# Another order of the heads in the first attention, and another quarter of V kept in SBUF

## The chip, the cores and the metric

The kernel runs on one core of a Trainium2 chip. The metric is the time of one execution on the device, in microseconds (us).

## The reference

Four tokens (B = 4, one position each, D = 512) go through two layers, each an attention with a cached K and V and a gated feed-forward block. Both layers use the same weights and the same cache:

```python
x = x + A(layernorm(x)); x = x + B(layernorm(x))     # first layer
x = x + A(layernorm(x)); x = x + B(layernorm(x))     # second layer

def A(x):      # 32 query heads in groups of 4 on 8 KV heads, Dh = 128, the last W = 2048 positions
    q = x @ wq
    o = softmax(q k^T * Dh ** -0.5) @ v
    return o @ wo
def B(x):      # F = 1792
    return (sigmoid(x @ w_gate) * (x @ w_up)) @ w_down
```

K of one KV head, for all four batches, is 2 MB in bf16, and so is V. wq and wo are 4 MB each, the three weights of B 1.75 MB each.

## The kernel before, in words

The program is written as a plan (`_Plan`): each operation names its engine, an estimated length, and what it reads and writes. `_schedule` then puts the operations of each engine in a fixed order by running the plan with these estimates: at each step it takes, among the operations that could start within 60 ns of the earliest one, the one that stands first in the program. The issues of DMAs (all on SP, line 461) keep the order of the program. `_assign_sync` turns the dependencies into semaphore waits. On the chip each engine runs its list in order, and so an instruction that waits holds up all that stand behind it on its engine.

SBUF is filled by hand. A place is written as (buffer, first unit, units); a unit is 256 bf16 values in each of 128 partitions, 64 KB. The buffers are:

- `kt`: K of all eight heads, 32 units each (256 units). It is read from memory once, transposed in place by TensorE and copied back (lines 736 and 746), and used by both layers.
- `ws` (`wo_sb`): wo, 8 units per head, kept for both layers.
- `ar` (`arena`, 75 units) and `sx` (`side`, 31 units): everything that streams, V, wq and the weights of B, and parts of these that stay.

`WHERE` says which places each load takes; names are `V0_h` for V of head h in the first attention, `V2_h` in the second, `g`, `u` and `d` for the gate, up and down weights, `q01` for the half of wq that is read twice.

**First attention** (layer 0). The loop goes over `HEADS1`. For each head it transposes K of the next one, makes the scores (`scores`, line 759), softmax (maximum line 768, exponential line 781, transpose of the result lines 787 and 792), the product with V (`pv_wo`) and the product with wo (line 947). V of head h lies in the arena in one of two slots of 32 units, units 42 to 73 and units 0 to 31, in turns. In the last place of the order, V comes in three pieces.

**Feed-forward block** (`glu`). Its gate weights and the second reading of wq need room in `ws`, where wo lies. So `stash` copies 16 units of wo into four PSUM banks (VectorE, line 994), and copies them back (ScalarE, line 990) before the second attention uses them.

**Second attention** (layer 2). K is in `kt` already. V is read again, except for pieces that are still where the first attention left them: `VKEEP` names, for a head, the unit of its V at which such a piece starts, and `load_v` leaves out its DMA and puts it first in the list of pieces of the product. Before: for head 6 its last quarter (8 units, in arena units 66 to 73), and for head 7 its last 6 units (arena units 30 to 35). V of heads 0 and 1 goes to free parts of the arena and `side`. V of heads 2 to 7 overwrites K in `kt`, from the bottom up: the load of V of head 2 waits for the scores of head 0, and so on, two heads behind. The loop `for n, h in enumerate(HEADS2)` makes the scores of head n, issues the load of V of head n + 1, does the product with V and wo of head n - 2 (`v2_head`), and spreads the softmax weights of head n.

The product with V has two forms. In `WIDE` places (heads 2 to 5 in the second attention) it is one group of 32 matmuls of 256 columns (line 852), copied out by ScalarE (line 860) and summed by TensorE (line 867); it needs the whole of V. In the others (heads 0, 1, 6 and 7) it is 64 matmuls of 32 columns (line 895), one group for each piece of V, so that a piece can be used as soon as it is there.

After the second attention comes the last `glu`, whose down weights lie in the arena (`d0_3`), in `kt` behind V of head 7 (`d4_3`, `d8_3`) and in `side` (`d12_3`), and the output.

Of the kernel before, what the change touches and what calls it, by code (L numbers as in the profile page):

```python
# [268 lines left out]
def build(nc, A_x, A_k, A_v, A_wq, A_wo, B_wg, B_wu, B_wd, out):  # L269
# [4 lines left out]
    _, HKV, SK, DH = A_k.shape  # L274
# [23 lines left out]
    UHEAD = NB * UBLK  # L298
    KEEPG = 4
    GU = F // UNIT  # L300
# [4 lines left out]
    AHEAD = 2  # L305
    NWR = 7
    WIDE = {0: {0: 4, 1: 4, 2: 4, 3: 4, 4: 4, 5: 4, 6: 2}, 2: {2: 2, 3: 2, 4: 2, 5: 2}}
    VKEEP = {6: 24, 7: 26}
    HEADS1 = list(range(HKV))
    HEADS2 = list(range(HKV))  # L310

    SCRATCH = 256
# [10 lines left out]
    NS = (low - SIDE) // (2 * UNIT)  # L323
# [15 lines left out]
    with es:  # L339
        def sb(name, shape, dt):  # L340
            return es.enter_context(nc.sbuf_tensor(name, shape, dt))

        kt = sb("kt", [128, HKV * NB * BLK], BF16)
# [12 lines left out]
        pb = sb("pb", [128, 4 * UNIT], BF16)  # L356
# [48 lines left out]
        def blk_ap(s):  # L405
            return {"kt": kt, "ws": wo_sb, "ar": arena, "pt": pt, "pb": pb, "sx": side}[s[0]][:, s[1] * UNIT:(s[1] + s[2]) * UNIT]

        def blk_tok(s):
            return tuple((s[0], u) for u in range(s[1], s[1] + s[2]))

        def kblk(h, b):
            return ("kt", (h * NB + b) * UBLK, UBLK)
# [6 lines left out]
        MAIN = WKEEP[2][0][1]  # L419
        G0 = MAIN - KEEPG * GU  # L420

        def ar(u, n):
            return ("ar", u, n)

        def sx(u, n):
            return ("sx", u, n)

        WHERE = {}
        for h in range(HKV - 1):
            WHERE["V0_%d" % h] = [ar(MAIN - UHEAD if h % 2 == 0 else 0, UHEAD)]  # L430
        WHERE["V0_%d" % (HKV - 1)] = [ar(0, 16), ar(16, 10), ar(30, 6)]
        WHERE["u01"], WHERE["g01"] = ar(52, 2 * GU), ar(38, 2 * GU)
        PT3 = ("kt", 187, 4)
        WHERE.update({
            "g23_1": ("ws", 0, 2 * GU), "u23_1": ar(0, 2 * GU),
            "d0_1": ar(14, 8), "d4_1": ar(22, 8), "d8_1": ar(36, 2), "d9_1": ("ws", 14, 2), "d10_1": ("pb", 0, 4),
            "d12_1": ("pt", 4, 4),
            "q01": [("ws", 0, 8), ar(0, 14), ar(14, 4), ("ws", 8, 6)],
            "V2_0": [ar(18, 12), ar(36, 2), sx(0, 16), sx(16, 2)],
            "V2_1": [sx(18, NS - 18), ar(0, 18), ar(74, 1)],  # L440
            "g23_3": ar(0, 2 * GU), "u23_3": sx(0, 2 * GU),
            "d0_3": ar(14, 8), "d4_3": ("kt", 179, 8), "d8_3": ("kt", 192, 8), "d12_3": sx(14, 4),
        })
        WHERE["V2_6"] = [("kt", 128, 24), ar(66, 8)]
        WHERE["V2_7"] = [("kt", 152, 16), ("kt", 168, 10), ar(30, 6)]
        for h in range(2, HKV - 2):
            WHERE["V2_%d" % h] = [("kt", (h - 2) * UHEAD, UHEAD)]

        def bankb(b):
            return ps[:, b, :].bitcast(BF16)  # L450
# [7 lines left out]
        def dma(name, dst, src, w, r=(), rate="bw_4k", nbytes=None, sem=None):  # L458
            if nbytes is None:
                nbytes = dst.partition_size() * dst.free_nbytes()  # L460
            o = P.op("sync", name, 0.0, lambda e, dst=dst, src=src: e.dma_start(dst, src),
                     r=r, w=w, dma_bytes=nbytes, dma_rate=tm[rate])
            if sem is not None:
                o.sem = sem
                o.inc = 16
            return o

        def load_v(L, h):
# [3 lines left out]
            for s in WHERE["V%d_%d" % (L, h)]:  # L472
                n = s[2]
                if L == 2 and VKEEP.get(h) == u0:
                    got.insert(0, (s, u0 * UNIT // 128))
# [247 lines left out]
        def k_head(h, banks):  # L723


            base = h * NB * BLK
            for t in range(UBLK):
                bank, ev = banks[tcount[0] % len(banks)]
                tcount[0] += 1

                def e_tr(pe, t=t, bank=bank):
                    last = None
                    for v in range(2):
                        for q in range(NB):
                            c0 = base + (q * NJ + 2 * t + v) * 128
                            last = pe.transpose(bankb(bank)[:, (v * NB + q) * 128:(v * NB + q + 1) * 128],  # L736
                                                kt[:, c0:c0 + 128], ident_b[:, :])
                    return last
                tok = [("kt", (h * NB + b) * UBLK + t) for b in range(NB)]
                P.op("tensor", "T%d_%d" % (h, t), 8 * tm["pe_tr"], e_tr,  # L740
                     r=tok + [("ident_b",)], w=[("pst", bank)], banks=(bank,))

                def e_ev(e, ev=ev, t=t, bank=bank):
                    to = kt[:, base:base + NB * BLK].rearrange("p (b y) -> p b y", b=NB)[:, :, t * UNIT:(t + 1) * UNIT]
                    fr = bankb(bank)[:, 0:NB * UNIT].rearrange("p (y b) -> p b y", b=NB)
                    return (e.tensor_copy if ev == "vector" else e.copy)(to, fr)  # L746
                P.op(ev, "evT%d_%d" % (h, t), 1300.0 if ev == "vector" else 1100.0, e_ev,
                     r=[("pst", bank)], w=tok, banks=(bank,))
# [231 lines left out]
                 r=[("pswt",), ("xT",)], w=[("xT",)], banks=(MB,))  # L980

        GB, UB, YB = 0, 1, 2
        STASH = ((0, 3), (4, 0), (8, 1), (12, 2))

        def stash(back):
            for u, b in STASH if back else STASH[1:] + STASH[:1]:
                at = blk_ap(("ws", u, 4))
                r, w = [("wo", u * UNIT // WOH)], [("st", b)]
                if back:
                    P.op("scalar", "back%d" % u, 1010.0, lambda a, b=b, at=at: a.copy(at, bankb(b)), r=w,  # L990
                         w=r + list(blk_tok(("ws", u, 4))), banks=(b,))
                else:
                    P.op("vector", "stash%d" % u, 620.0,
                         lambda v, b=b, at=at: v.tensor_scalar(ps[:, b, :].bitcast(I32), at.bitcast(I32), 0, None, ALU.bitwise_or),
                         r=r, w=w + [("pst", b), ("pss", b)] + list(blk_tok(("ws", u, 4))), banks=(b,))
# [142 lines left out]
        TBK = [(i % 3, "vector" if i % 8 in (1, 4, 7) else "scalar") for i in range(24)]  # L1138
# [19 lines left out]
        def load_k(h):  # L1158
            dma("K_%d" % h, kt[:, h * NB * BLK:(h + 1) * NB * BLK], k_d[h],
                w=[t for b in range(NB) for t in blk_tok(kblk(h, b))], rate="bw_16k", nbytes=NB * W * DH * 2)  # L1160
# [7 lines left out]
                dma("wo_%d" % h, to, A_wo[h * REP * 128:(h + 1) * REP * 128, :].rearrange("(p j) n -> p (j n)", j=4),  # L1168
                    w=[("wo", h)])

        load_k(0)
        k_head(0, TBK)
        pieces = []
        for ktc in range(2):
            s = ("kt", HKV * UHEAD - (2 - ktc) * 2 * UBLK, 2 * UBLK)
# [11 lines left out]
        for n in range(1, KLEAD):  # L1187
            load_k(HEADS1[n])
        for n, h in enumerate(HEADS1):
            if n + 1 < HKV:  # L1190
                k_head(HEADS1[n + 1], TBK)
            scores(0, n, h, 3, MB)
# [3 lines left out]
            if n + KLEAD < HKV:  # L1196
                load_k(HEADS1[n + KLEAD])
            if n == HKV - 1:
# [76 lines left out]
def bass_interleave_layers__sliding_block_cached__glu_gated_glu__decode_kernel(  # L1275
    nc, A_x, A_k_cache, A_v_cache, A_wq, A_wo, B_x, B_w_gate, B_w_up, B_w_down, out,
):
    build(nc, A_x, A_k_cache, A_v_cache, A_wq, A_wo, B_w_gate, B_w_up, B_w_down, out)
# [28 lines left out]
```

## Time and profile before

| what | us |
|---|---|
| median of 3 runs | 176.73 (176.54 to 176.75) |
| the profiled execution's own time | 177.9 |
| its span in the profile | 176.1 |
| TensorE (PE) busy | 136.4 |
| VectorE (DVE) busy | 99.7 |
| ScalarE (ACT) busy | 75.6 |
| first instruction of the second attention's scores (L759) | starts at 124.0 |
| output DMA issued | 173.9 |

Times in the views run from the start of the span. In rows of the timeline the columns are start, length (both us), engine, line of the kernel, operation, what it writes and reads, shapes, and how many instructions are merged; in brackets stands how long the engine was idle before, and what ended that. SPq stands for a DMA issue on SP. A row of the DMA issues gives the size and the median time from issue to landing. PEclk is the clock that was granted to TensorE, 1 being full.

### The profile page before, as it was taken

The numbers are of one execution on the slowest core, as the hardware profiler recorded it, in microseconds if no ns is written. First come the engines' busy times: TensorE is split into PE (matmuls) and PEld (weight loads), VectorE is DVE, ScalarE is ACT, GpSimd is POOL, SyncE is SP. The second block draws the span as 40 slices with busy tenths as digits, with TensorE's granted clock in tenths as the row PEclk, the third lists the DMA queues.
The fourth block names the chain that finished last, engine by engine and source line by source line (L and its number), as shares of the span: only waits on it lengthen the run. The fifth ranks groups of instructions, "written<-read, shape, count | busy, mean of one in ns | idle before, by whom it ended". The sixth has DMA issues, their size and how long they took to land.

```text
span 176.1 us, 4872 instructions
## 1 busy us (share of the span) xinstructions
PE 136.4 (77%) x2175; PEld 99.8 (57%) x2175; DVE 99.7 (57%) x246; ACT 75.6 (43%) x129; POOL 6.8 (4%) x17
## 2 busy tenths in 40 slices
PE   0394699898897878978977967459849796897794
PEld 0382398566385664665654657448227553675693
DVE  7453016969658576894797532104499888521440
ACT  2073227947287647292663040304455644430300
POOL 5200000000000000000000002002000000000020
PEclk9999557999999999999999555555599999655555
DMA  5999999999999999999999999999899999999930
GB/s 187 417 436 437 422 421 421 443 424 422 421 421 432 414 431 424 411 432 422 434 424 381 408 422 412 396 407 399 305 411 430 435 435 417 421 411 419 401 153 5
DMA packets 9504, 69.39 MB, mean 394 GB/s; under 512 B 1032, under 2 KB 2316, under 8 KB 6156
## 3 DMA queue, kind: packets, MB, share of 16 engines
q1 hardware_dynamic: 9476, 69.08, 94.8%
q8 instruction: 17, 0.28, 0.6%
q14 instruction: 3, 0.02, 0.0%
q10 hardware_dynamic: 8, 0.00, 0.0%
HBM read 69.08 MB, written 0.00 MB: 392 GB/s over the span
## 4 chain that ended last, share of the span: by engine, by line
DMA 62%; PE 29%; DVE 3%; ACT 3%; issue 1%; SPq 1%; DVEq 0%
DMA arena<-in_A_v_cache_dram 31%; DMA kt<-in_A_v_cache_dram 11%; DMA side<-in_A_wq_dram 9%; PE ps L852 6%; DMA wo_sb<-in_B_w_gate_dram 5%; DMA wo_sb<-in_A_wq_dram 5%; PE ps L759 4%; PE ps L736 4%; PE ps L1050 3%; PE ps L668 2%; PE ps L867 2%; PE ps L895 2%; PE ps L947 1%; ACT wo_sb L990 1%; PE ps L699 1%
## 5 line engine op out<-in xcount | busy, mean ns | idle before, releaser
L746 ACT COPY kt<-ps 128x1024 bf16<-128x1024 bf16 x40 | 39.1, 1018 | 25.7 <-PE ps L736 25.6
L736 PE MATMUL ps<-ident_r,kt 128*128 128x128 bf16 x512 | 38.5, 231 | 4.8 <-DMA kt<-in_A_k_cache_dram 2.6
L736 PEld LDWEIGHTS ps<-ident_r,kt 128*128 128x128 bf16 x512 | 32.7, 105 | 11.7 <-issue 4.4
L746 DVE COPY kt<-ps 128x1024 bf16<-128x1024 bf16 x24 | 29.2, 1215 | 12.5 <-PE ps L736 12.3
L759 PE MATMUL ps<-kt,qs 128*32 128x512 bf16 x256 | 18.0, 405 | 2.0 <-ACT pb L781 1.3
L817 DVE TENSOR_TENSOR pt<-ps,ofbr 128x1024 bf16<-128x1024 f32 (+1 forms) x15 | 15.5, 1031 | 2.9 <-PE ps L792 2.8
L852 PE MATMUL ps<-arena,pt 128*64 128x512 bf16 (+1 forms) x128 | 13.4, 391 | 4.3 <-DMA arena<-in_A_v_cache_dram 4.2
L768 DVE TENSOR_REDUCE nmz<-ps 128x1 f32<-128x512 f32 x16 | 11.0, 687 | 6.1 <-PE ps L759 5.9
L781 ACT ACTIVATE pb<-ps,nmz 128x512 bf16<-128x512 f32 x16 | 11.1, 693 | 7.2 <-DVE nmz L778 3.7
L787 DVE STREAM_TRANSPOSE pb<-pb 128x512 bf16<-128x512 bf16 x16 | 11.3, 704 | 4.4 <-ACT pb L781 4.2
L852 PEld LDWEIGHTS ps<-arena,pt 128*64 128x64 bf16 (+1 forms) x128 | 6.0, 117 | 9.7 <-DMA arena<-in_A_v_cache_dram 5.7
L759 PEld LDWEIGHTS ps<-kt,qs 128*32 128x32 bf16 x256 | 5.6, 100 | 7.7 <-ACT pb L781 1.9
L860 ACT COPY arena<-ps 128x512 f32<-128x512 f32 (+1 forms) x7 | 3.9, 556 | 13.8 <-PE ps L852 13.8
L824 ACT ACTIVATE pt<-ps,ofbr 128x96 bf16<-128x96 f32 x28 | 7.2, 342 | 5.4 <-PE ps L792 5.3
L630 POOL TENSOR_TENSOR rs<-pt,rs 128x4 f32<-128x4 f32 x4 | 4.1, 1014 | 119.9 <-DVE pt L626 119.9
L832 PE MATMUL ps<-rowf,nmz 128*128 128x16 f32 x32 | 6.8, 290 | 2.1 <-DVE pt L817 1.9
L947 PE MATMUL ps<-wo_sb,onr 128*16 128x512 bf16 x56 | 6.5, 457 | 2.0 <-DVE onr L939 2.0
L867 PEld LDWEIGHTS ps<-arena 128*128 128x128 f32 x52 | 6.7, 201 | 2.1 <-ACT arena L860 1.6
L867 PE MATMUL ps<-arena 128*128 128x16 f32 x52 | 7.4, 273 | 0.7 <-ACT arena L860 0.2
L1050 PE MATMUL ps<-xn,arena 128*128 128x5 bf16 (+1 forms) x168 | 6.3, 172 | 2.0 <-DMA arena<-in_B_w_up_dram 1.1
L832 PEld LDWEIGHTS ps<-rowf,nmz 128*128 128x128 f32 x32 | 5.4, 212 | 4.1 <-DVE pt L817 2.8
L990 ACT COPY wo_sb<-ps 128x1024 bf16<-128x1024 bf16 x4 | 4.0, 1012 | 8.3 <-DMA wo_sb<-in_A_wq_dram 8.3
(143 smaller groups left out, 161.1 us busy)
## 6 DMA issues: line engine op xcount, KB each, us to landing
kt<-in_A_k_cache_dram SPq DMA_DIRECT2D x8, 2048.0 KB, 24.5
arena<-in_A_v_cache_dram SPq DMA_DIRECT2D x7, 2048.0 KB, 20.2
kt<-in_A_v_cache_dram SPq DMA_DIRECT2D x4, 2048.0 KB, 18.3
wo_sb<-in_A_wo_dram SPq DMA_DIRECT2D x8, 512.0 KB, 25.2
kt<-in_A_wq_dram SPq DMA_DIRECT2D x1, 2048.0 KB, 11.6
side<-in_A_wq_dram SPq DMA_DIRECT2D x1, 1984.0 KB, 15.7
arena<-in_B_w_up_dram SPq DMA_DIRECT2D x2, 896.0 KB, 7.8
arena<-in_B_w_gate_dram SPq DMA_DIRECT2D x2, 896.0 KB, 14.2
```

Of the source, the lines that this page charges most:

```text
L736: last = pe.transpose(bankb(bank)[:, (v * NB + q) * 128:(v * NB + q + 1) * 128], kt[:, c0:c0 + 128], ident_b[:, :])
L746: return (e.tensor_copy if ev == "vector" else e.copy)(to, fr)
L759: last = pe.matmul(ps[32 * b:32 * b + 32, sbk, 0:CB * 128], qs[:, q0:q0 + 32], blk_ap(kblk(h, b))[:, c * CB * 128:(c + 1) * CB * 128], sta ...
L768: lambda v: v.tensor_reduce(nmv, ps[:, sbk, 0:CB * 128], AXX, ALU.max, negate=True),
L781: o = a.activation(pbuf[:, :], ps[:, sbk, 0:CB * 128], ACTF.Exp, bias=gv, scale=1.0, accum_out=zv)
L787: P.op("vector", "ptr%d_%d" % (L, h), 650.0, lambda v: v.transpose(turned[:, :], pbuf[:, :]), r=[("pb", 0), ("pb", 1)], w=[("pb", 2), ("pb ...
L817: lambda v: v.tensor_tensor(pv4[:, 0:nj], spread(tbk, nj).unsqueeze(2).broadcast_to([128, nj, NB, REP]), ofb[:, :].unsqueeze(1).unsqueeze( ...
L832: lambda pe: pe.matmul(ps[:, tbk, CB * NQ:CB * NQ + NR], zv.broadcast_to([128, 128]), rowf[:, :], start=True, stop=True),
L852: last = pe.matmul(ps[rows * g:rows * (g + 1), bank, 0:wide * 128].rearrange("p (c d) -> p c d", c=wide), ptv[:, w0:w0 + rows], v, start=( ...
L867: last = pe.matmul(ps[:, out[0], out[1]:out[1] + NR], part[:, c * 128:(c + 1) * 128], ey[wide][:, c * NR:(c + 1) * NR], start=(c == 0), st ...
L947: last = pe.matmul(ps[32 * j:32 * j + NR, WB, 0:D], onr[:, j * NR:(j + 1) * NR], wo_sb[:, h * WOH + j * D:h * WOH + (j + 1) * D], start=(n ...
L1050: last = pe.matmul(ps[:, bank, fc * wid:(fc + 1) * wid], cols[:, fc - g0, :], xn[:, ktc * (NB + 1):ktc * (NB + 1) + wid], start=(ktc == 0 ...
```

## The change

Six things change together.

- `HEADS1` becomes 1, 2, 3, 4, 5, 6, 0, 7. The slots of V in the arena now go by the place in that order, so V of head 0 lies in the slot that V of head 6 had, and is the last one there.
- `VKEEP` names head 0 in place of head 6: the last quarter of V of head 0 (8 units, arena units 66 to 73) stays for the second attention.
- V of head 0 in the second attention: 24 units are loaded (12 and 2 in the arena, 8 and 2 in `side`) and the kept 8 are used in place. Before, all 32 were loaded (12, 2, 16 and 2).
- V of head 1 takes the place that this frees in `side` (21 units in place of 13) and 11 in place of 19 units of the arena.
- V of head 6 is loaded whole, in two halves of 16 units. With that it takes 8 more units of `kt`, so V of head 7 moves up by 8, and two loads of down weights move into the place of K of head 6.
- The 16 units of wo that are put away are those of heads 1 and 2, the first two of the new order, in place of heads 0 and 1. The gate weights, a part of w_down and the parts of wq that lie in `ws` move along by 8 units.

```diff
-    VKEEP = {6: 24, 7: 26}
-    HEADS1 = list(range(HKV))
+    VKEEP = {0: 24, 7: 26}
+    HEADS1 = list(range(1, HKV - 1)) + [0, HKV - 1]
...
-        for h in range(HKV - 1):
-            WHERE["V0_%d" % h] = [ar(MAIN - UHEAD if h % 2 == 0 else 0, UHEAD)]
+        for n in range(HKV - 1):
+            WHERE["V0_%d" % HEADS1[n]] = [ar(MAIN - UHEAD if n % 2 == 0 else 0, UHEAD)]
...
-            "g23_1": ("ws", 0, 2 * GU), "u23_1": ar(0, 2 * GU),
-            "d0_1": ar(14, 8), "d4_1": ar(22, 8), "d8_1": ar(36, 2), "d9_1": ("ws", 14, 2), "d10_1": ("pb", 0, 4),
+            "g23_1": ("ws", 8, 2 * GU), "u23_1": ar(0, 2 * GU),
+            "d0_1": ar(14, 8), "d4_1": ar(22, 8), "d8_1": ar(36, 2), "d9_1": ("ws", 22, 2), "d10_1": ("pb", 0, 4),
...
-            "q01": [("ws", 0, 8), ar(0, 14), ar(14, 4), ("ws", 8, 6)],
-            "V2_0": [ar(18, 12), ar(36, 2), sx(0, 16), sx(16, 2)],
-            "V2_1": [sx(18, NS - 18), ar(0, 18), ar(74, 1)],
+            "q01": [("ws", 8, 8), ar(0, 14), ar(14, 4), ("ws", 16, 6)],
+            "V2_0": [ar(18, 12), ar(36, 2), sx(0, 8), sx(8, 2), ar(66, 8)],
+            "V2_1": [sx(10, NS - 10), ar(0, 11)],
+            "V2_6": [("kt", 128, 16), ("kt", 144, 16)],
+            "V2_7": [("kt", 160, 16), ("kt", 176, 10), ar(30, 6)],
             "g23_3": ar(0, 2 * GU), "u23_3": sx(0, 2 * GU),
-            "d0_3": ar(14, 8), "d4_3": ("kt", 179, 8), "d8_3": ("kt", 192, 8), "d12_3": sx(14, 4),
+            "d0_3": ar(14, 8), "d4_3": ("kt", 192, 8), "d8_3": ("kt", 200, 8), "d12_3": sx(14, 4),
         })
-        WHERE["V2_6"] = [("kt", 128, 24), ar(66, 8)]
-        WHERE["V2_7"] = [("kt", 152, 16), ("kt", 168, 10), ar(30, 6)]
...
-        STASH = ((0, 3), (4, 0), (8, 1), (12, 2))
+        STASH = ((8, 3), (12, 0), (16, 1), (20, 2))
...
-        load_k(0)
-        k_head(0, TBK)
+        load_k(HEADS1[0])
+        k_head(HEADS1[0], TBK)
```

## The prediction

> **What bounds the kernel now.** I read the page first, for the load of each engine and of the DMA stream.
>
> ```profile
> span 176.1 us, 4872 instructions
> PE 136.4 (77%) x2175; PEld 99.8 (57%) x2175; DVE 99.7 (57%) x246; ACT 75.6 (43%) x129; POOL 6.8 (4%) x17
> PEclk9999557999999999999999555555599999655555
> DMA  5999999999999999999999999999899999999930
> HBM read 69.08 MB, written 0.00 MB: 392 GB/s over the span
> DMA 62%; PE 29%; DVE 3%; ACT 3%; issue 1%; SPq 1%; DVEq 0%
> ```
>
> The DMA engines are full from the first slices to the last two, and 62% of the chain is a wait for a transfer. The change moves no byte out of the program: a quarter of V of head 0 (512 KB) is no longer read twice, a quarter of V of head 6 now is. So the stream's length is not what changes; what changes is when each piece of it lands. Next I read the chain in order of time, for the place where DMA stops being the bound.
>
> ```profile
> 129.74 19.84 DMA kt<-in_A_v_cache_dram
> 149.63 1.06 PE ps L852 x32
> ...
> 173.63 0.29 DVE pb L1132
> ```
>
> The last transfer in the chain is V of head 4 of the second attention (V2_4), landing at 149.6. From there to 173.9 the chain holds only engine work. So the end moves with the landing of V2_4, unless the 24 us behind it change too. The timeline of PE in this stretch shows both the waits and the work behind them.
>
> ```profile
> 139.67 1.06 PE L852 MATMUL ps<-kt,pt 128*32 128x256 bf16 x32 [0.88 <-DMA kt<-in_A_v_cache_dram]
> 142.92 1.05 PE L759 MATMUL ps<-kt,qs 128*32 128x512 bf16 x16
> 143.90 0.30 PE L932 MATMUL ps<-onb,ident_r 128*128 128x16 bf16 x4
> 144.65 1.06 PE L852 MATMUL ps<-kt,pt 128*32 128x256 bf16 x32 [0.22 <-DMA kt<-in_A_v_cache_dram]
> 149.63 1.06 PE L852 MATMUL ps<-kt,pt 128*32 128x256 bf16 x32 [1.38 <-DMA kt<-in_A_v_cache_dram]
> 150.83 0.29 PE L792 MATMUL ps<-pb,perm 128*128 128x96 bf16 x2
> 153.98 0.63 PE L895 MATMUL ps<-pt,arena 128*128 128x32 bf16 x16
> 154.54 1.90 PE L852 MATMUL ps<-kt,pt 128*32 128x256 bf16 x32
> 159.60 1.46 PE L895 MATMUL ps<-pt,kt 128*128 128x32 bf16 x48
> 162.50 1.03 PE L895 MATMUL ps<-kt 128*128 128x32 bf16 x32
> 164.30 0.69 PE L895 MATMUL ps<-kt 128*128 128x32 bf16 x20
> ```
>
> The four L852 groups are the PV products of heads 2 to 5 (PV2_2 to PV2_5). The first three wait 0.88, 0.22 and 1.38 us for V, 2.48 in all. The starts at 139.67 and 144.65 are 4.98 apart, each on a landing of 2 MB (2.10 MB / 4.98 us = 421 GB/s). The 16 matmuls at 153.98 are the kept quarter of head 6, done early because it lies in SBUF already; the 48 at 159.60 are the rest of head 6; the 32 and 20 are head 7. Last, the issues of V and the final weights, each with its time to landing.
>
> ```profile
> 132.73 0.54 SPq L461 DMA_DIRECT2D kt<-in_A_v_cache_dram  x1
> kt<-in_A_v_cache_dram SPq DMA_DIRECT2D x1, 2048.0 KB, 21.8
> ...
> 135.74 0.54 SPq L461 DMA_DIRECT2D kt<-in_A_v_cache_dram  x1
> kt<-in_A_v_cache_dram SPq DMA_DIRECT2D x1, 1536.0 KB, 22.5
> ...
> 142.21 0.54 SPq L461 DMA_DIRECT2D kt<-in_A_v_cache_dram  x1
> kt<-in_A_v_cache_dram SPq DMA_DIRECT2D x1, 1024.0 KB, 18.5
> ...
> 147.81 4.09 SPq L461 DMA_DIRECT2D side<-in_B_w_down_dram  x1
> side<-in_B_w_down_dram SPq DMA_DIRECT2D x1, 256.0 KB, 23.2
> 173.13 0.45 PE L1119 MATMUL ps<-side,pt 128*25 128x128 bf16 x8
> ```
>
> V2_5 lands at 154.5, V2_6 at 158.2, the first part of V2_7 at 160.7, the last weight piece at 171.0. Against the uses above, V2_5 has no slack, V2_6 1.4 us, V2_7 1.8, the last weights 2.1.
>
> **The change, part by part.** *First attention in the order 1 to 6, 0, 7.* Loads of K, V and wo keep their sizes and places in the queue, slots alternate by position, and the widths of PV go by position too. No instruction is added or removed: 0 us, covered by a stream that carries the same bytes in the same steps. *The stash and its copies back.* They move from units 0 to 15 of wo_sb to units 8 to 23, the same four copies in the same PSUM banks.
>
> ```profile
> 119.69 1.01 ACT L990 COPY wo_sb<-ps 128x1024 bf16<-128x1024 bf16 x1 [6.54 <-DMA wo_sb<-in_A_wq_dram]
> 145.02 2.75 SPq L461 DMA_DIRECT2D kt<-in_B_w_down_dram  x2
> 125.98 0.54 SPq L461 DMA_DIRECT2D kt<-in_A_v_cache_dram  x1
> ```
>
> The copies back still wait for the same two wq pieces, whose order and sizes stay: 0 us. *w_down moved within kt.* Its first piece there now overwrites K of head 6 and not of head 5, so SP waits for scores 6 (142.92 plus 1.05) and not scores 5. SP issues it at 145.02, a microsecond after that: 0 us. If scores 6 came later by up to 2 us, three weight loads (this one, its fellow and the last side piece) would stand behind the wait; the last was issued 23.2 us ahead of its landing, so that is hidden too. The w_up load into side now also needs PV of head 1, done before 139.67: hidden.
>
> *512 KB leave V2_0 and join V2_6.* V2_2 is issued at 125.98, when scores 0 free K of head 0; nothing in the change makes that earlier. But 512 KB less lie ahead of it in the queue. At 421 GB/s (0.524 MB) V2_2 to V2_5 land **1.25 us** earlier; V2_6, now full, and everything behind it land when they did. PV2_4 can then start at 148.38 and not 149.63. That this shift arrives in full needs a queue that is never empty, which these stretches bear on (columns: PE, PEld, DVE, ACT, POOL busy, then granted clock, DMA share, GB/s).
>
> ```profile
> 124.00:126.00 2.00, 1.97 (x21) 0.59 (x22) 0.01 (x1) 1.51 (x2) 0.00 (x0) 0.50 0.95 320
> 126.00:128.00 2.00, 1.77 (x28) 0.71 (x26) 1.79 (x7) 0.18 (x1) 0.00 (x0) 0.69 0.73 267
> 128.00:130.00 2.00, 1.26 (x18) 0.44 (x18) 1.80 (x6) 0.72 (x3) 0.00 (x0) 1.00 1.02 421
> 148.00:150.00 2.00, 0.62 (x19) 0.51 (x22) 1.91 (x7) 0.16 (x2) 0.10 (x1) 1.00 1.03 442
> 150.00:152.00 2.00, 1.96 (x38) 1.45 (x26) 0.82 (x1) 1.26 (x6) 0.00 (x0) 0.78 1.00 428
> 152.00:154.00 2.00, 1.58 (x14) 1.01 (x15) 1.18 (x4) 0.79 (x3) 0.00 (x0) 0.50 0.98 412
> ```
>
> At 126 to 128 the stream sinks to 267 GB/s, a share of 0.73: some of the 16 engines had run dry. So the price of the shift lies between 1.25 (only engines that were ahead ran dry) and 0 (the freed 1.25 us become a longer dip). I take 1.25: from V2_2 on a landing comes every 4.98 us without a hole, so the engine that lands last had work throughout.
>
> *The kept quarter moves from head 6 to head 0.* PV of head 0 has the same 64 matmuls. PV of head 6 no longer has 16 that can be done at 153.98, ahead of V2_5, where they cost nothing (V2_5 landed at 154.5). They go behind V2_6's data: 16 x (1.46 / 48) = **0.49 us** on the path. The halves of V2_6 soften this: the first lands 2.5 us before 158.2 and can fill PE's small waits. I keep 0.49, with 0 as the other end.
>
> *PE's order.* Instructions are put in order by the planner, which among ready ones takes the earliest in the program. PV of head 3 stands ahead of scores 6 in the program, yet PE did scores 6 first (142.92), since V2_3 was due only later. With V2_3 due 1.25 earlier, PV2_3 probably goes first, and then PE, which gets there 0.88 sooner (142.04), waits for V2_3 at 143.40: 1.36 us with scores 6, and all of head 6's softmax, queued behind. Counting PE alone: it reached PV2_4 at 148.25; without its two earlier waits (0.88 and 0.22) 147.15, with the new wait 148.51. That is 0.13 later than V2_4's landing at 148.38, so the flip costs **0.13** there. Not counted is the softmax of head 6: scores 6 would start about 1.9 later.
>
> The sum: 1.25 - 0.13 - 0.49 = 0.63 us faster. PV2_6 then starts at 158.48, still behind V2_6 at 158.2. The profiled execution took 177.9 us (span 176.1, 1.8 around it), the median of the runs is 176.73; the span would become 175.5, that execution 177.3, the median **176.1**. About 0.2% (0.35 us) is what a measurement here can tell from no change. This case runs from 175.9 (no flip, 0.76, and a little of the 0.49 hidden) to 176.4.
>
> **The rivals.** *Handed back.* The flip's delay reaches PE again through softmax.
>
> ```profile
> 148.74 0.65 DVE L787 STREAM_TRANSPOSE pb<-pb 128x512 bf16<-128x512 bf16 x1
> ```
>
> This transpose of head 6 ends at 149.39, and PE takes its product at 150.83: 1.44 us of slack. Scores 6 coming 1.9 later uses all of it and 0.46 more, so the product of head 6 starts at about 151.3 while PE would be there at 149.7. PE can fill part of that with the sums of head 4; then PV2_5 gains about half of the 1.12, which the 0.49 takes: 176.7. For it: DVE is busy 1.91 of 2 us at 148 to 150, so it can't catch up. Against it: other work can move into the hole.
>
> *Slower: the queue runs dry before V2_2.* Place: 124 to 128. If the dip deepens by the 1.25 us of bytes that are taken away, V2_2 lands at 139.6 as before, no wait shrinks, and V2_6 lands at 159.5. PE comes to head 6 at 159.60 as before, now with 64 matmuls: +0.49, 177.2. It decides from the point at which the slowest DMA engine, and not only those ahead, has nothing between 124 and 128. The dip speaks for it, the even landings from 139.6 against it. The softmax delay in full would end at the same time (0.46 more than now, and half of the 0.49 hidden).
>
> *Faster: the clock stays up.* In the windows, PE is busy 0.62 of 2 us at 148 to 150, waiting for V2_4, and then the granted clock falls from 1.00 to 0.50. The same 32 matmuls of L852 take 1.06 at the full clock and 1.90 at half. If the wait shrinks and one more stretch of some 3.4 us (what separates the wait from the full drop) stays at full clock, PV2_5 saves 0.84, and the 1.58 us of PE work at 152 to 154 would halve: 0.79. Of these 1.63, with data that allow 1.8 (V2_7), I take 1.5: 175.2. The Trainium skill (TensorE: Matmul & The Clock Gate, What's actually happening) says that the clock halves after an idle window of about 3.4 us and that the windows run freely; by that rule a shorter wait can keep it up, and a new wait at 142 to 143.4 can drop it sooner. The trace agrees in that the drop follows the emptiest stretch; how empty is enough, it doesn't show.
>
> **How the numbers follow.** Forecast 0.35, handed back 0.28, slower 0.24, clock 0.13. The first lies partly within 0.2% of no change, so faster gets 0.45, same 0.30, slower 0.25. The range 175.2 to 177.2 reaches to both outer cases; the likeliest one's own is 175.9 to 176.4.
>
> **What would show it.** Right: PV2_2 waits less than 0.2 us, PV2_4 starts near 148.5 and PV2_5 near 153.4, and two groups of 32 matmuls of L895 on kt end near 160.4. The flip: L852 of head 3 before the second-last L759 group. Slower: L852 of head 2 still on a landing near 139.6 and less than 267 GB/s at 126 to 128. Clock: L852 of head 5 near 1.1 us. The forecast is wrong if PV2_5 is no earlier than 154.2, or if the time before 124 us moves by more than 0.3.

## The result, and the profile after

The changed kernel takes 175.79 us in the median (174.60 to 177.61, 22 runs) against 176.81 for the kernel before (22 runs). The ratio is 0.9908, interval 0.9884 to 0.9931: 1.2 to 2.1 us faster, most likely 1.6; it is formed from the runs within 1.5% of the fastest of the same kernel. The medians alone are only 1.0 us apart: 11 runs of the kernel before lie at 176.4 to 176.8 and 11 from 176.9 up, and its median sits at the edge of the lower group. e4 below, the same two kernels timed once more, has 0.9902. The forecast was 176.1 by a gain of 0.63. The sign is right; the forecast gain is less than half of the measured one. The profiled execution took 176.48 us, with a span of 174.6.

The page of the changed kernel, as it was read before:

```profile
span 174.6 us, 4868 instructions
PE 139.6 (80%) x2175; PEld 102.3 (59%) x2175; DVE 99.5 (57%) x246; ACT 75.4 (43%) x129; POOL 6.8 (4%) x17
PEclk9999755999999987999999755555555999955555
DMA  5999999999999999999999999999999999999940
DMA 54%; PE 33%; DVE 5%; ACT 4%; SPq 1%; issue 1%; DVEq 0%; ACTq 0%
```

The DMA row has no 8 left at slice 29, and DMA's share of the chain falls from 62% to 54%. The chain in order of time shows which part went (start, length, engine, line):

```profile
119.65 1.02 ACT wo_sb L990
...
124.00 1.93 PE ps L759 x16
...
152.44 0.40 PE ps L832 x2
152.84 0.32 PE ps L947 x4
153.16 1.73 PE ps L852 x32
...
172.19 0.29 DVE pb L1132
```

No transfer of the second attention's V stands in it any more: from 119.65 on it holds only engines, where the kernel before waited for V2_4 until 149.63. The scores of head 0 start at 124.00, as before, so nothing ahead of them moved. PE's timeline in the stretch of the prediction's rows:

```profile
140.96 1.06 PE L852 MATMUL ps<-kt,pt 128*32 128x256 bf16 x32
...
142.50 1.05 PE L759 MATMUL ps<-kt,qs 128*32 128x512 bf16 x16
...
144.09 1.06 PE L852 MATMUL ps<-kt,pt 128*32 128x256 bf16 x32
...
145.64 1.05 PE L759 MATMUL ps<-kt,qs 128*32 128x512 bf16 x16
...
148.69 0.83 PE L852 MATMUL ps<-kt,pt 128*32 128x256 bf16 x23
...
152.44 0.40 PE L832 MATMUL ps<-rowf,nmz 128*128 128x16 f32 x2 [0.50 <-DVE pt L817]
...
152.99 1.88 PE L852 MATMUL ps<-kt,pt 128*32 128x256 bf16 x32
...
156.21 1.01 PE L895 MATMUL ps<-pt,kt 128*128 128x32 bf16 x32
...
158.58 1.03 PE L895 MATMUL ps<-pt,kt 128*128 128x32 bf16 x32
...
161.05 1.03 PE L895 MATMUL ps<-kt 128*128 128x32 bf16 x32
```

None of the four wide products waits for V; before, three waited 2.48 us in all. For PV2_2 that isn't the landing alone: PE came to it 1.3 us later than before (140.96 and 139.67), in an execution whose granted clock was 0.50 until 136, where the one before had 1.00 from 128 on. The order has flipped as foretold (PV2_3 at 144.09, scores 6 at 145.64). The clock still falls, since PV2_5 takes 1.88. Head 6 ends at 159.61 (158.58 plus 1.03) and not at 161.06. The issues of V2_2 and V2_5 in the timeline of SP, and then their rows among the DMA issues, give their landings, start plus time to landing (137.7 and 152.3):

```profile
125.94 0.54 SPq L461 DMA_DIRECT2D kt<-in_A_v_cache_dram  x1
...
134.43 0.54 SPq L461 DMA_DIRECT2D kt<-in_A_v_cache_dram  x1
```

```profile
kt<-in_A_v_cache_dram SPq DMA_DIRECT2D x1, 2048.0 KB, 11.8
...
kt<-in_A_v_cache_dram SPq DMA_DIRECT2D x1, 2048.0 KB, 17.9
```

Both come some 2 us earlier than before, not 1.25. And the windows at 124 to 130 (last columns granted clock, DMA share, GB/s) show from where:

```profile
124.00:126.00 2.00, 2.00 (x22) 0.64 (x23) 0.05 (x1) 1.51 (x2) 0.00 (x0) 0.50 1.01 411
126.00:128.00 2.00, 2.00 (x28) 0.68 (x25) 1.58 (x6) 0.22 (x1) 0.00 (x0) 0.50 0.98 414
128.00:130.00 2.00, 1.53 (x20) 0.45 (x16) 1.74 (x5) 0.55 (x2) 0.00 (x0) 0.50 1.09 445
```

The dip of the kernel before (320 and 267 GB/s) is gone. At 421 GB/s those four us would have moved 0.51 MB more (2 x 101 plus 2 x 154 KB): 1.2 us of stream that the kernel before lost and the changed one does not. The last weights, with the same bytes ahead of them in both kernels, landed 1.0 us earlier, which is the nearer measure.

### The profile page after: what moved, and what is told of

Same layout as the page of the kernel before. It is cut to its first block, busy times and chain, and to the rows that moved or that the text cites. A ratio compares the mean times of both kernels' runs of the same rounds, so it can differ in the third digit from the quotient of the medians.

```text
span 174.6 us, 4868 instructions
## 1 busy us (share of the span) xinstructions
PE 139.6 (80%) x2175; PEld 102.3 (59%) x2175; DVE 99.5 (57%) x246; ACT 75.4 (43%) x129; POOL 6.8 (4%) x17
## 4 chain that ended last, share of the span: by engine, by line
DMA 54%; PE 33%; DVE 5%; ACT 4%; SPq 1%; issue 1%; DVEq 0%; ACTq 0%
DMA arena<-in_A_v_cache_dram 31%; DMA kt<-in_A_k_cache_dram 12%; PE ps L852 7%; PE ps L759 7%; DMA wo_sb<-in_B_w_gate_dram 6%; DMA wo_sb<-in_A_wq_dram 5%; PE ps L736 4%; PE ps L1050 3%; PE ps L895 3%; PE ps L867 2%; SPq L461 1%; PE ps L832 1%; PE ps L947 1%; ACT pb L781 1%; ACT pt L824 1%
## 5 line engine op out<-in xcount | busy, mean ns | idle before, releaser
L736 PE MATMUL ps<-ident_r,kt 128*128 128x128 bf16 x512 | 40.6, 240 | 5.4 <-DMA kt<-in_A_k_cache_dram 3.2
L736 PEld LDWEIGHTS ps<-ident_r,kt 128*128 128x128 bf16 x512 | 35.3, 111 | 12.1 <-issue 4.0
L759 PE MATMUL ps<-kt,qs 128*32 128x512 bf16 x256 | 20.4, 448 | 1.3 <-DVE qs L715 0.7
L817 DVE TENSOR_TENSOR pt<-ps,ofbr 128x1024 bf16<-128x1024 f32 (+1 forms) x15 | 15.4, 1030 | 2.7 <-PE ps L792 2.6
L852 PE MATMUL ps<-arena,pt 128*64 128x512 bf16 (+1 forms) x128 | 12.7, 361 | 3.1 <-DMA arena<-in_A_v_cache_dram 3.1
L832 PE MATMUL ps<-rowf,nmz 128*128 128x16 f32 x32 | 7.3, 304 | 2.3 <-DVE pt L817 2.2
L1050 PEld LDWEIGHTS ps<-xn,arena 128*128 128x128 bf16 x168 | 6.3, 118 | 2.2 <-DMA arena<-in_B_w_up_dram 1.2
```

The lines of the kernel that those rows point to most:

```text
L759: last = pe.matmul(ps[32 * b:32 * b + 32, sbk, 0:CB * 128], qs[:, q0:q0 + 32], blk_ap(kblk(h, b))[:, c * CB * 128:(c + 1) * CB * 128], sta ...
L817: lambda v: v.tensor_tensor(pv4[:, 0:nj], spread(tbk, nj).unsqueeze(2).broadcast_to([128, nj, NB, REP]), ofb[:, :].unsqueeze(1).unsqueeze( ...
L832: lambda pe: pe.matmul(ps[:, tbk, CB * NQ:CB * NQ + NR], zv.broadcast_to([128, 128]), rowf[:, :], start=True, stop=True),
L852: last = pe.matmul(ps[rows * g:rows * (g + 1), bank, 0:wide * 128].rearrange("p (c d) -> p c d", c=wide), ptv[:, w0:w0 + rows], v, start=( ...
L1050: last = pe.matmul(ps[:, bank, fc * wid:(fc + 1) * wid], cols[:, fc - g0, :], xn[:, ktc * (NB + 1):ktc * (NB + 1) + wid], start=(ktc == 0 ...
```

## The experiments

Each was timed in five rounds beside the kernel before, on the same chip as it; the four groups e1 to e4, e5 to e8, e9 to e11 and e12 to e15 were timed apart. The table has every kernel, with the landings of one profiled execution (issue plus time to landing), the ratio to the kernel before with its interval, and the fastest run.

| kernel | V2_2 | V2_5 | V2_6 | last weights | ratio | fastest, us |
|---|---|---|---|---|---|---|
| before | 139.6 | 154.5 | 158.3 | 171.0 | 1 | 176.1 to 176.6 |
| changed | 137.7 | 152.3 | 157.3 | 170.0 | 0.9908 [0.9884, 0.9931] | 174.6 |
| e1 before again | 139.8 | 154.9 | 158.6 | 171.3 | 1.0007 [0.9968, 1.0045] | 176.4 |
| e2 before, less | 137.9 | 152.5 | 156.4 | 169.1 | 0.9891 [0.9838, 0.9944] | 174.3 |
| e3 changed, reload | 138.4 | 153.1 | 158.3 | 171.4 | 0.9994 [0.9963, 1.0024] | 176.3 |
| e4 changed again | 137.4 | 152.1 | 157.1 | 169.8 | 0.9902 [0.9867, 0.9937] | 174.9 |
| e5 before, split | 138.8 | 153.5 | 157.2 | 170.2 | 0.9977 [0.9935, 1.002] | 175.5 |
| e6 changed, merged | 137.1 | 151.7 | 156.8 | 169.8 | 0.9903 [0.9862, 0.9944] | 174.6 |
| e7 before, kept last | 140.0 | 154.7 | 158.5 | 171.2 | 1.0009 [0.9975, 1.0043] | 176.4 |
| e8 changed, V2_6 whole | 138.1 | 152.7 | 157.6 | 170.3 | 0.99 [0.9869, 0.9931] | 175.2 |
| e9 reload, short tail | 138.7 | 153.4 | 158.3 | 169.8 | 0.9965 [0.9929, 1.0002] | 176.3 |
| e10 changed, long tail | 137.5 | 152.1 | 157.1 | 171.1 | 0.9895 [0.9846, 0.9944] | 175.5 |
| e11 before, filled wait | 140.1 | 154.8 | 158.5 | 171.2 | 0.9987 [0.9948, 1.0026] | 176.6 |
| e12 changed, V2_6 late | 137.3 | 152.0 | 158.6 | 171.3 | 0.9948 [0.992, 0.9975] | 176.0 |
| e13 reload, V2_6 early | 138.3 | 153.8 | 157.6 | 170.3 | 0.9939 [0.9897, 0.9982] | 175.1 |
| e14 changed, no flip | 137.1 | 152.5 | 157.5 | 170.2 | 0.989 [0.9848, 0.9933] | 174.9 |
| e15 merged, 24 and 8 | 137.2 | 151.8 | 157.0 | 169.7 | 0.9908 [0.9876, 0.994] | 174.7 |

### Is it the landings?

*e1* is the kernel before and *e4* the changed one, run once more beside the others. *e2* takes 512 KB away from V2_0 in the kernel before, without the new order and without the halves. *e3* loads the kept quarter of the changed kernel again.

```diff
 e2, against the kernel before (8 units of V2_0 are not read)
-    VKEEP = {6: 24, 7: 26}
+    VKEEP = {0: 24, 6: 24, 7: 26}
-            "V2_0": [ar(18, 12), ar(36, 2), sx(0, 16), sx(16, 2)],
+            "V2_0": [ar(18, 12), ar(36, 2), sx(0, 8), sx(16, 2), sx(8, 8)],
 e3, against the changed kernel
-    VKEEP = {0: 24, 7: 26}
+    VKEEP = {7: 26}
```

> The kernel before, unchanged, for a second profile and the clock of each of its runs. If the dip of the DMA stream at 124 to 128 us (267 GB/s) belongs to the program, it stands here again and V of head 4 lands within 0.3 us of 149.6; if it was that one execution's, V of head 4 lands near 148.6. If the granted clock explains the gain, runs of before at the clock of the faster runs of after (0.83) are as short as those, 174.7; if the landings explain it, runs of before stay at 176.4 or more at any clock.

> The kernel before, but the last 512 KB of V of head 0 are not loaded in the second attention (the product uses what lies in those 8 units of side, so the output isn't the reference's); the kept quarter of head 6 stays. All landings behind come 1.25 us earlier, nothing else changes. If the earlier landings of V of heads 2 to 5 are the cause, the time is that of after, 175.8, or 0.3 less, since no matmul moves behind V of head 6. If the clock or the new order of the heads is the cause, it stays within 0.3 of 176.7.

> The kernel after, but the kept quarter of V of head 0 is loaded again to the same place (512 KB more in all). The new order of the heads, the halves of V of head 6 and the 16 matmuls behind it stay. If the earlier landings are the cause, V of heads 2 to 5 lands 1.25 us later than in after and the time goes to 176.8 to 177.3, as before or above it. If the order, the halves or the clock are the cause, it stays at 175.8.

> The kernel after, unchanged, for a second profile on the same chip. If the dip at 124 to 128 us is gone because of the change, it is absent again and V of head 4 lands within 0.3 us of 147.45 and the last weight piece within 0.3 of 170.0. If its absence was chance, it may be back and these land 1 us later.

e2 alone brings the whole gain (0.9891), e3 takes it away (0.9994). So the order of the heads as such is worth nothing that can be measured, and the time is a matter of when bytes land. Yet e3 raised a question: its V2_2 lands 1.2 us earlier than in the kernel before, with the same bytes ahead of it, and it wins nothing.

### The dip

The window at 126 to 128 (last columns clock, DMA share, GB/s) is low in every profile of a kernel with V2_0 as before (220 to 267 GB/s in before, e1, e7 and e11); here in e1:

```profile
126.00:128.00 2.00, 2.00 (x32) 0.80 (x28) 1.63 (x6) 0.10 (x1) 0.00 (x0) 0.50 0.79 253
```

In e3, with as many bytes ahead of V2_2, it is not:

```profile
126.00:128.00 2.00, 2.00 (x24) 0.56 (x21) 1.47 (x6) 0.33 (x1) 0.00 (x0) 0.50 1.06 432
```

One thing that differs is the load of 16 units (1 MB) into `side`. *e5* issues it as two of 8 units in the kernel before, *e6* makes one of 10 units of the changed kernel's 8 and 2, so that it waits for both pieces of wq there.

```diff
 e5
-            "V2_0": [ar(18, 12), ar(36, 2), sx(0, 16), sx(16, 2)],
+            "V2_0": [ar(18, 12), ar(36, 2), sx(0, 8), sx(8, 8), sx(16, 2)],
 e6
-            "V2_0": [ar(18, 12), ar(36, 2), sx(0, 8), sx(8, 2), ar(66, 8)],
+            "V2_0": [ar(18, 12), ar(36, 2), sx(0, 10), ar(66, 8)],
```

> The kernel before with the 1 MB load of V2_0 into side issued as two of 512 KB; bytes and order stay. Theory 'hole': the dip to 267 GB/s at 126 to 128 comes from this one large load, which is issued late because it waits for both wq pieces in side. Then the dip goes, V2_2 lands near 138.4 in place of 139.6 to 139.8, and the ratio to before is 0.993 to 0.995. Rival 'bytes': only the 512 KB that are left out move V2_2; then the dip stays or moves nothing, V2_2 lands at 139.6 or later and the ratio is 0.999 to 1.001.

> The changed kernel with its two side loads of V2_0 (512 and 128 KB) issued as one of 640 KB, which then waits for both wq pieces; bytes stay. Theory 'hole': the dip comes back, V2_2 lands near 138.4 to 138.7 in place of 137.4 to 137.7, and the ratio to before is 0.995 to 0.997. Rival 'bytes': V2_2 stays at 137.4 to 137.7 and the ratio at 0.990 to 0.991.

The same window in e5:

```profile
126.00:128.00 2.00, 1.74 (x27) 0.63 (x23) 1.73 (x7) 0.27 (x1) 0.00 (x0) 0.69 1.02 389
```

And in e6:

```profile
126.00:128.00 2.00, 2.00 (x28) 0.69 (x25) 1.59 (x6) 0.21 (x1) 0.00 (x0) 0.50 0.99 393
```

In both the dip is gone. With e5 everything behind it lands about a microsecond earlier (V2_2 at 138.8 and not 139.6 to 140.1), at the same bytes: the dip belonged to the 1 MB load. The wait for both wq pieces alone doesn't make it, since e6's 640 KB wait for both without a dip. Nor does the size alone: in the kernel before, the 1 MB of V2_7 landed 2.5 us behind V2_6 (158.2 and 160.7), at the full rate. Why this one load leaves DMA engines idle and two of 512 KB in its place don't stays open; size and wait together aren't excluded, as e5's first half waits for one piece only. Of e5's time (0.9977) the interval holds both no gain and the full microsecond; its one profiled execution took 176.86 and that of the kernel before 177.9, both with PV2_5 at half clock (1.90).

### Terms of the sum: the 16 matmuls, the halves, the flip

```diff
 e7, kernel before: the kept quarter of head 6 last in its product
-                    got.insert(0, (s, u0 * UNIT // 128))
+                    got.insert(0 if h == 7 else len(got), (s, u0 * UNIT // 128))
 e8, changed kernel: V2_6 in one load
-            "V2_6": [("kt", 128, 16), ("kt", 144, 16)],
+            "V2_6": [("kt", 128, 32)],
 e14, changed kernel: PV2_3 ranked behind scores 6
-                 r=blk_tok(s) + pk + (("pa", kp),), w=[("pvw", bank)], banks=(bank,))
+                 ..., prio=len(P.ops) + 40 if (L, n) == (2, 3) else None)
```

> The kernel before with the kept quarter of V of head 6 taken last in its product and not first: 16 matmuls move behind the landing of V2_6, as the prediction had it for the change. Theory of the prediction: they cost their 0.49 us on the path; PV2_6 becomes one group of 64 after the landing near 158.3, and the ratio is 1.002 to 1.004. Rival: the matmuls before the landing left PE waiting anyway, and the ratio is 0.999 to 1.001.

> The changed kernel with V2_6 loaded in one piece of 2 MB and not in two halves. Theory: the halves let 32 matmuls of head 6 run before the second half's landing (157.1 to 157.3); without them all 64 start there, PE ends head 6 about 1 us later, and the ratio to before is 0.994 to 0.996. Rival: PE gets to head 6 too late for the halves to matter, and the ratio stays at 0.990 to 0.991.

> The changed kernel with the product of head 3 ranked 40 places later in the planner's choice, so that scores 6 go ahead of it on PE as in the kernel before; transfers stay. Theory of the prediction: the flip cost 0.13 us at head 4, so the ratio is 0.989 to 0.990, a tenth of a us below the changed kernel. Rival 'flip pays': the order with the product first is what keeps PE from waiting for V2_4, and the ratio goes up to 0.993 to 0.996.

e7 moves the 16 matmuls behind the landing (the rest of PE's order stays, but for the last 20 matmuls of head 7, which move up by one place) and costs 0.2 us with an interval from -0.4 to 0.8: the prediction's 0.49 lies in it, and so does nothing. e8 shows no price for the whole V2_6 in its ratio, though PE waited 1.45 us for it in the profiled execution and the fastest run (175.2) lies behind those of the changed kernel (174.6 and 174.9). e14 has the order of the kernel before (scores 6 at 143.38, PV2_3 at 144.92) on the landings of the changed one, and is no slower: the flip neither pays nor costs anything that can be measured. By the ratios, none of the three carries the missing microsecond.

### The tail and the clock

e9 leaves out 512 KB of the last down weights in the kernel of e3, e10 adds 512 KB there to the changed kernel; e11 fills PE's wait for V2_4 in the kernel before with repeats of a matmul that stands there.

```diff
 e9
+            if (L, fc0) != (3, 8): dma("wd%d_%d" % (L, fc0), ...)
 e10
+            (L, fc0) == (3, 8) and dma("extra", blk_ap(("kt", 208, 8)), rows, ...)
 e11, line 832, for head 5 of the second attention
-                 lambda pe: pe.matmul(ps[:, tbk, ...], ..., stop=True),
+                 lambda pe: [pe.matmul(ps[:, tbk, ...], ..., stop=True) for _ in range(4 if (L, n) == (2, 5) else 1)][-1],
```

> The changed kernel with the quarter of V of head 0 loaded again (as in the run after_reload) and with one piece of the last down weights (512 KB) not loaded, so the output of the last block is made from what lies there; bytes ahead of V2_2 are as many as before, bytes of the whole stream as many as in the changed kernel. Theory 'stream end': V2_2 to V2_5 already came early enough in the reloaded kernel, and what held its time at 0.999 was the landing of the last weights (171.4). Then the last weights land near 170.1 and the ratio is 0.990 to 0.993. Rival 'V2 landings': V2_2 at 138.4 and V2_5 at 153.1 set the time, and the ratio stays at 0.996 to 1.000.

> The changed kernel with 512 KB more, read into a free place of kt just ahead of the last but one piece of the down weights; V2_2 to V2_7 land as in the changed kernel, the last weights 1.2 us later (near 171.1). Theory 'stream end': the ratio goes to 0.995 to 0.998. Rival 'V2 landings': it stays at 0.990 to 0.992, since the last weights still land ahead of their use.

> The kernel before with the matmul of line 832 for head 5 done four times over, in the 1.4 us in which PE waits for V2_4; every transfer and the order stay. Theory 'clock': the idle stretch is what takes the clock down near 151, ahead of PV2_5; with it filled, PV2_5 takes 1.06 and not 1.90, and the ratio is 0.992 to 0.996. Rival 'no clock': the granted clock falls at the same place, or its fall costs nothing, and the ratio is 0.999 to 1.001.

The end of the stream is not the bound: with the last weights at 171.1, where the kernel before has them, e10 keeps the whole gain (0.9895). The clock alone isn't either. Runs of the kernel before at a mean clock of 0.83 or more took 176.35 to 178.37 us (18 runs), those of the changed kernel 174.63 to 175.69 (8 runs), and over all their runs with a clock on record (119 and 32) the mean is the same within 0.001 (0.815). In e11's timeline the filler ends the wait, PV2_5 runs at the full clock (1.06), and then PE stands before the next landing:

```profile
149.04 1.04 PE L832 MATMUL ps<-rowf,nmz 128*128 128x16 f32 x8
150.01 1.06 PE L852 MATMUL ps<-kt,pt 128*32 128x256 bf16 x32
...
154.84 1.06 PE L852 MATMUL ps<-kt,pt 128*32 128x256 bf16 x32
...
158.55 1.41 PE L895 MATMUL ps<-pt,kt 128*128 128x32 bf16 x48 [0.27 <-DMA kt<-in_A_v_cache_dram]
```

The bracket names V2_6. That is the bound which the prediction had left in its place. The full clock needn't be the filler's work: PV2_5 takes 1.06 in e7 too.

### V2_5 and V2_6 apart

e12 moves V2_6 back to where the kernel before has it, and leaves V2_5 early. e13 does the reverse to the kernel of e3: V2_5 as there, V2_6 earlier.

```diff
 e12, ahead of the loads of V2_6
+                (L, h, u0) == (2, 6, 0) and dma("extra", blk_ap(ar(22, 8)), v_d[h][:, :, 0:8 * UNIT], ...)
 e13, second load of V2_6: 8 of its 16 units
```

> The changed kernel with 512 KB more, read into a free place of the arena just ahead of V2_6; V2_2 to V2_5 land as in the changed kernel, V2_6 and all behind it 1.2 us later (V2_6 near 158.4, as in the kernel before). Theory 'two bounds': the end follows the later of PV2_5's end and V2_6's landing, and V2_6 must come earlier too for the gain; then the ratio goes to 0.995 to 0.998. Rival 'V2_5 alone': it stays at 0.989 to 0.992.

> The reloaded kernel (the quarter of V of head 0 read again) with 8 of the last 16 units of V2_6 not loaded, so head 6 of the second attention is made from what lies there; V2_2 to V2_5 land as in the reloaded kernel (V2_5 near 153.2), V2_6 1.2 us earlier (near 157.1). Theory 'two bounds': V2_6 was what held the reloaded kernel at 0.997 to 0.999; the ratio goes to 0.990 to 0.994. Rival 'V2_5 alone': the ratio stays at 0.996 to 0.999.

PE's timeline in e12, from PV2_5 to the second half of head 6:

```profile
152.06 1.90 PE L852 MATMUL ps<-kt,pt 128*32 128x256 bf16 x32 [0.46 <-DMA kt<-in_A_v_cache_dram]
...
156.20 1.04 PE L895 MATMUL ps<-pt,kt 128*128 128x32 bf16 x32 [0.74 <-DMA kt<-in_A_v_cache_dram]
...
158.67 1.04 PE L895 MATMUL ps<-pt,kt 128*128 128x32 bf16 x32
```

e12's timeline waits 0.74 us for the first half of V2_6, and the second starts at 158.67 on a landing of 158.6. With V2_5 2.5 us early and V2_6 held, 0.5% is won; with V2_6 free as well, 1.0% (e10, whose V2_5 lands as early; the intervals overlap). From the other side, e13 (0.9939) doesn't decide: it lies below e3 (0.9994) and e9 (0.9965), whose V2_6 is late, but the intervals touch, V2_5 came at 153.8 in its profile, later than meant, and the medians of all its runs and of those beside it (177.37 and 177.90) give 0.997.

The profiled executions tell more than these ratios. Both landings bind, now the one and now the other, and the clock decides which. Where PV2_5 ran at half clock (1.88 to 1.92 us: before, e1, e5, changed, e10, e14, e15), PE came to the last matmuls that need V2_6 0.4 to 1.4 us after its landing, and the span ended 21.5 to 22.0 us behind the start of PV2_5, over starts from 152.2 to 154.9. Where it ran at full clock (1.05 or 1.06: e2, e4, e6, e7, e8, e11), PE started them within 0.1 us of the landing, and the span ended 16.1 to 16.8 us behind that, over landings from 156.4 to 158.5. e12 is the exception at half clock (held by V2_6), e13 at full clock (0.8 us behind it); e3 and e9 lie between (1.39 and 1.44). In e4, the changed kernel at full clock, with V2_6 landed at 157.1:

```profile
152.14 1.06 PE L852 MATMUL ps<-kt,pt 128*32 128x256 bf16 x32
...
157.13 1.04 PE L895 MATMUL ps<-pt,kt 128*128 128x32 bf16 x32
```

The last column of the table agrees, more roughly: the fastest run of each kernel comes 17.3 to 18.4 us behind its V2_6, over landings that differ by 2.2 us; behind V2_5 it comes 21.3 to 24.0.

*e15* asked for more of it, with both side loads merged and 16 matmuls behind the last landing of V2_6.

```diff
-            "V2_6": [("kt", 128, 16), ("kt", 144, 16)],
+            "V2_6": [("kt", 128, 24), ("kt", 152, 8)],
```

> The changed kernel with V2_0's two side loads as one of 640 KB and V2_6 in pieces of 24 and 8 units, so that 16 matmuls and not 32 stand behind its last landing. Theory 'two bounds': where the clock is up, V2_6's landing sets the end, and 0.3 to 0.5 us come off; the ratio is 0.986 to 0.989. Rival: the time is set elsewhere, and the ratio stays at 0.990.

It stays at 0.9908. In its profile PE got to head 6 at 157.43, with V2_6 landed at 157.0. No version here beats the changed kernel by more than its interval.

## Why the prediction came out too small

*The sign was right, the time of PV2_4 by luck.* PV2_2 no longer waits, the flip came, PV2_4 starts at 148.69 (foretold: near 148.5) and PV2_5 at 152.99 (near 153.4). Nothing moved before 124. But the prediction came to 148.5 by a new wait of 1.36 us that ends with V2_3 at 143.40. No such wait came: V2_3 landed at 142.6, and PE got to it only at 144.09, its clock having been half until 136. In e4, where the clock was up from 130, there was no wait either (V2_3 at 142.3, PE at 143.06), and PV2_4 starts at 147.65.

*The step that failed is the landing shift: "V2_2 to V2_5 land 1.25 us earlier; V2_6, now full, and everything behind it land when they did".* V2_2 and V2_5 landed 1.9 and 2.2 us earlier, V2_6 1.0 and the last weights 1.0. The prediction saw the dip at 126 to 128, and priced it from one side only: it could eat the 1.25 us or not. That the dip itself, 1.2 us of stream worth by its own two rows, belonged to the 1 MB load which the change cuts to 512 KB was not among the cases. e5 shows it at the same bytes, and e3 with the changed kernel's pieces.

*The sum, term by term, in the two profiled executions* (both with PV2_5 at half clock). PV2_5 starts 1.55 us earlier (154.54 and 152.99), where 1.25 less 0.13 for the flip made 1.12: 0.43 more, from the landings. From there to the end of head 6 takes 6.62 us and 6.52 before, 0.10 more, where 0.49 was put for the 16 matmuls: 0.39 less. So head 6 ends 1.45 us earlier and not 0.63, and the executions are 1.42 us apart.

*V2_6 was taken as a cover with 1.4 us of slack.* It had that slack in the one profile, where PV2_5 ran at half clock. Where PV2_5 takes 1.06, as in e11, the slack is gone and V2_6 is next. e12 is near the prediction's own case, V2_6 unmoved and V2_5 early (by 2.5 us and not 1.25): 0.9948, a gain of 0.4 to 1.4 us, which holds its 0.63. In such executions V2_6's microsecond is the part that the prediction hadn't.

*The 0.49 for the 16 matmuls was the upper end.* The first half of V2_6 ran at 156.21, ahead of the last product with wo of head 5, so that 32 matmuls and not 64 stood behind it; 0.10 us of the 0.49 is left in the profiled pair. By time it can't be told from nothing (e7, e8). The 0.13 of the flip can't either (e14).

*The rivals.* The queue that runs dry before V2_2 went the other way: the dip vanished. Of "handed back" a part came: V2_5 had landed at 152.3, but PE reached it at 152.99, behind a matmul that waited 0.50 us for VectorE's weights of head 6 (L817). The clock rival was wrong as put: PV2_5 took 1.88 in the profile of the changed kernel and 1.06 in e4, the same kernel once more, so the clock there goes with the execution and not with the change; e7, with V2_2 to V2_6 as late as before, has 1.06 too. The prediction's 3.4 us between the wait and the drop aren't in the rows: by the 0.78 at 150 to 152 the clock fell near 151.1, 2.9 us behind the start of the wait at 148.25. And e11, with the wait for V2_4 filled, gains no more than its interval allows, 0.9 us.

## What to carry to other kernels

A stretch where a saturated stream sinks can be a cost of the layout in front of it: work out its bytes (here 0.51 MB, 1.2 us), find the load it stands behind, and count its end as one of the cases whenever a change resizes that load. A landing with slack in one profile is not covered if the slack comes from a slow clock; list the next landing at the full clock as well. And when bytes move from ahead of one landing to ahead of another, hold one and move the other: e10 and e12, which differ in where 512 KB more stand in the queue, show the price of V2_6's landing best. Compare profiles at the same clock: at half and at full clock another landing binds.

## What the runs showed of the hardware

- At one place in the queue, a load of 1 MB into 128 partitions cost the stream 0.8 to 1.3 us against two of 512 KB, with the same bytes (V2_2 at 139.6 to 140.1 against 138.8; 220 to 267 GB/s for 2 us against 389). Elsewhere in the same kernel, in V2_7, 1 MB landed 2.5 us behind the load ahead of it, without a loss.
- The mean granted clock differed between runs of one kernel from 0.79 to 0.84, and the time went with it: a line through the runs of the changed kernel falls by 35 us per unit of clock, so by 1.75 us over that range, as much as the change itself. In the kernel before the line is less clear (25 us per unit, correlation -0.4), and e8, e11 and e12 show none. The Trainium skill (TensorE: Matmul & The Clock Gate, What's actually happening) says that the activity windows run freely and puts the price of a ramp under 1% of a span; here the spread that goes with the clock reaches 1%.
- The clock also falls without an idle window. The same section has it halve after an idle window of 3.4 us; in the changed kernel PE was busy 1.75 and 1.77 of 2 us ahead of the fall at 153:

```profile
148.00:150.00 2.00, 1.75 (x46) 1.08 (x42) 1.93 (x8) 1.39 (x5) 0.24 (x1) 1.00 0.99 414
150.00:152.00 2.00, 1.77 (x25) 1.17 (x13) 1.87 (x8) 1.24 (x6) 0.00 (x0) 1.00 0.98 414
152.00:154.00 2.00, 1.56 (x26) 1.19 (x30) 1.49 (x4) 1.14 (x5) 0.00 (x0) 0.76 1.03 422
```
